# Activation of the second stage in turns, its low parts on VectorE, GpSimd left out

## The chip, the core and the metric

The kernel runs on one core of a Trainium2 chip. Its engines work side by side, each through its own queue in order: PE (TensorE, matmuls; PEld is its weight load), DVE (VectorE), ACT (ScalarE), POOL (GpSimd) and SP (SyncE, which here issues every DMA). They wait for each other by semaphores. The metric is the time of one execution in microseconds; the median of several runs is given.

## The reference

```python
def _attn_ref(q, k, v, g_q, g_k):          # q, k, v: (8, 12, 448, 64)
    q_n, k_n = (rmsnorm(q, g_q), rmsnorm(k, g_k))
    scores = scale * np.matmul(q_n, k_n.transpose(0, 1, 3, 2))
    attn = softmax(scores)
    return np.matmul(attn, v)

def _moe_ref(x, w_in, w_out):               # x: (3584, 768), w_in: (768, 2048), w_out: (2048, 768)
    h = x @ w_in
    g = h * np.cos(h)
    return (g @ w_out).astype(np.float32)
```

x is the attention output with its heads joined. All is fp32. The change lies in `h * cos(h)` and around it.

## The kernel before

Matmuls run on pairs of rounded fp32 numbers: each operand is split into a high part (a cast to fp32r) and a low part (the rest), and three matmuls (high-high, high-low, low-high) take the place of one.

The first part of the program, up to about 1007 us, is the attention of eight batches with `h = x @ w_in` of the batch before in between; h goes to DRAM (`h_out` copies it from PSUM on ScalarE, `h_store` writes it). Then comes the second stage, written out by a second `Plan`: sixteen blocks of `h` of the last batch (`ffn1_block`, 18 matmuls each), and then `g @ w_out`.

The second product runs over four pairs of batches (b0, b1). A pair is done in seven products of the Strassen-Winograd form, P1, P5, P6, P2, P7, P3, P4 in this order. Each product has four groups, g = 0 to 3; a group is a block of 18 matmuls on PE, with operands 128 x 896. So a pair is 28 blocks or 504 matmuls, and the stage has 112 blocks or 2016 matmuls. The four quarters A, Bq, C, Dq of the activation are held in `gq[(q, g)]`. For each quarter and group:

- `gl_load` (SP, L523): loads h.
- `g_turns` step 0 (ACT, L528): n = h/2pi + 12582912, which rounds; step 1 (POOL, L530): takes the constant off and multiplies by -C1.
- `g_reduce` steps 0 and 1 (DVE, L535 and L537): h minus n times 2pi in two pieces, into r.
- `g_cos` (ACT, L541 and L542): the absolute value, then the sine of pi/2 minus it.
- `g_mul` (DVE, L545): times h.

`g_sum` (DVE, L548) makes differences of quarters, 16 groups a pair. For each block, `g_split` makes the high part (ACT, L556) and the low part (POOL, L554); the two rings of buffers for these hold four blocks each, the rings of n and r two. `ffn2` (PE, L576 to L578) takes both. A product ends in PSUM banks, three of eight; `o_copy` (ACT, L586) or `o_add` (DVE, L589) takes them out into `outs`, and `y_store` (SP, L592) stores the results. P6 takes one bank that P5 had: its third output waits for the first `o_add` of P5. `w_place` (SP, L564) loads weights; P5, P2, P3 and P4 use the same slots one after another.

What stands in which order on an engine is set by `Plan.order`, a list scheduler: every `add(engine, cost, due, function, ...)` is an instruction with a cost and a due time, and on each engine the ready one with the earliest due time goes next. Each engine then follows its list without exception.

Of the kernel before, what the change touches and what calls it, by code (L numbers as in the profile page):

```python
# [10 lines left out]
F32 = mybir.dt.float32  # L11
F32R = mybir.dt.float32r
I32 = mybir.dt.int32
AF = mybir.ActivationFunctionType
ALU = mybir.AluOpType
AX = mybir.AxisListType
PSUM = bass.MemoryType.PSUM

MAGIC = 12582912.0
C1 = 6.28125  # L20
C2 = 2.0 * math.pi - C1

TINY_SQ = 3.4332275390625e-05**2

PE, ACT, DVE, POOL, SP = "PE", "ACT", "DVE", "POOL", "SP"


class Plan:
# [18 lines left out]
    def add(self, eng, cost, due, fn, *args, r=(), w=(), land=0.0, start=0.0, lead=None):  # L47
        n = len(self.parts)
        deps = set()
        for key in r:  # L50
            deps.update(self.writer.get(key, ()))
        for key in w:
            deps.update(self.writer.get(key, ()))
            deps.update(self.readers.get(key, ()))
        for key in (*r, *w):
            name, inst = key[0], key[1]
            if name in self.rings:
                self.users.setdefault((name, inst), []).append(n)
        for key in r:
            self.readers.setdefault(key, []).append(n)  # L60
        for key in w:
            self.writer[key] = [n]
            self.readers[key] = []
        deps.discard(n)
        self.parts.append((eng, cost, due, fn, args, deps, land))
        self.start.append(start)
        self.lead.append(self.LEAD * (eng == PE) if lead is None else lead)
# [59 lines left out]
def tile_attention_moe(  # L127
# [11 lines left out]
    nc = tc.nc  # L139
    NU = sd_in.shape[0]  # L140
    B, S, D = 8, kT.shape[2], 64
# [9 lines left out]
    NG = 2  # L151
# [26 lines left out]
    halfpi = cpool.tile([128, 1], F32, tag="halfpi", name="halfpi")  # L178
# [311 lines left out]
    phs = {}  # L490
# [19 lines left out]

    def h_out(b, fc):
        he = hes[(b, fc)] = epool.tile([128, S], F32, tag="he", name=f"he{b}_{fc}")
        nc.scalar.copy(he, phs.pop((b, fc))[:, :S])  # L513

    def h_store(b, fc):
        nc.sync.dma_start(h_d[b, fc], hes.pop((b, fc)))
# [3 lines left out]
    gq, gns, grs, gsp = {}, {}, {}, {}  # L520
# [1 line left out]
    def gl_load(b, q, g, f0):  # L522
        nc.sync.dma_start(gq[(q, g)], h_d[b, f0 : f0 + NG].rearrange("f p s -> p f s"))  # L523

    def g_turns(i, q, g, step):
        if step == 0:
            gns[i] = gpool.tile([128, NG, S], F32, tag="n", name=f"n{i}", bufs=RING2["n"])
            nc.scalar.activation(gns[i], gq[(q, g)], AF.Copy, bias=MAGIC, scale=1.0 / (2.0 * math.pi))  # L528
        else:
            nc.gpsimd.tensor_scalar(gns[i], gns[i], -MAGIC, -C1, op0=ALU.add, op1=ALU.mult)  # L530

    def g_reduce(i, q, g, step):
        if step == 0:
            r = grs[i] = gpool.tile([128, NG, S], F32, tag="r2", name=f"r2{i}", bufs=RING2["r2"])
            nc.vector.tensor_tensor(r, gq[(q, g)], gns[i], ALU.add)  # L535
        else:
            nc.vector.scalar_tensor_tensor(grs[i], gns.pop(i), C2 / C1, grs[i], op0=ALU.mult, op1=ALU.add)  # L537

    def g_cos(i):
        r = grs[i]  # L540
        nc.scalar.activation(r, r, AF.Abs)  # L541
        nc.scalar.activation(r, r, AF.Sin, bias=halfpi, scale=-1.0)  # L542

    def g_mul(i, q, g):
        nc.vector.tensor_tensor(gq[(q, g)], grs.pop(i), gq[(q, g)], ALU.mult)  # L545
# [4 lines left out]
    def g_split(n, q, g, lo):  # L550
        t = gpool.tile([128, NG, S], F32R, tag="glo" if lo else "ghi", name=f"g{lo}_{n}", bufs=RING2["ghi"])
        gsp[(n, lo)] = t
        if lo:
            nc.gpsimd.tensor_tensor(t, gq[(q, g)], gsp[(n, 0)].bitcast(F32), ALU.subtract)  # L554
        else:
            nc.scalar.copy(t, gq[(q, g)])  # L556

# [22 lines left out]
    outs = {}  # L580
# [2 lines left out]
        outs["t"] = xpool.tile([128, 12, S], F32, tag="xs", name="outs")  # L583

    def o_copy(bank, dst):
        nc.scalar.copy(outs["t"][:, dst], banks[bank][:, :S])  # L586

    def o_add(bank, src, dst):
        nc.vector.tensor_tensor(outs["t"][:, dst], banks[bank][:, :S], outs["t"][:, src], ALU.add)  # L589

    def y_store(b, oc, src):
        nc.sync.dma_start(out[oc * 128 : oc * 128 + 128, b * S : (b + 1) * S], outs["t"][:, src])  # L592
# [3 lines left out]
    add = plan.add  # L596
# [182 lines left out]
    RING2 = {"he": 2, "n": 2, "r2": 2, "ghi": 4, "glo": 4}  # L779
# [7 lines left out]
    add = plan.add  # L787
# [35 lines left out]
    for t in range(B // 2):  # L823
        b0, b1 = 2 * t, 2 * t + 1
        T = T0 + 7 * NGR * BLOCK * t

        def produce(q, b, f0, due):
            nonlocal made
            for g in range(NGR):
                i, made = made, made + 1  # L830
                e = due + BLOCK * g
                k, nk, rk = ("G", q, g), ("n", i), ("r2", i)
                add(SP, ISS, e - 34.0, gl_load, b, q, g, f0 + NG * g, r=[("hd", b, f0 + NG * g + j) for j in range(NG)],
                    w=[k], land=LAND)
                add(ACT, 0.95, e - 24.0, g_turns, i, q, g, 0, r=[k], w=[nk])
                add(POOL, 1.35, e - 23.0, g_turns, i, q, g, 1, w=[nk])
                add(DVE, 1.4, e - 21.0, g_reduce, i, q, g, 0, r=[k, nk], w=[rk])
                add(DVE, 1.1, e - 20.0, g_reduce, i, q, g, 1, r=[nk], w=[rk])
                add(ACT, 2.0, e - 18.0, g_cos, i, w=[rk])
                add(DVE, 1.15, e - 15.0, g_mul, i, q, g, r=[rk], w=[k])  # L840

        def combine(dst, a, c, due):
            for g in range(NGR):
                add(DVE, 1.15, due + BLOCK * g - 13.0, g_sum, dst, a, c, g, r=[("G", a, g), ("G", c, g)], w=[("G", dst, g)])

        DUE = {name: T + NGR * BLOCK * k for k, (name, *_) in enumerate(PRODUCTS)}
        produce(A, b0, 0, DUE["P1"])
        produce(Bq, b1, 0, DUE["P5"])
        produce(C, b1, HF, DUE["P6"])
        produce(Dq, b0, HF, DUE["P2"])  # L850
        role = {}
        for k, (name, q, w0, bk, opens, closes) in enumerate(PRODUCTS):
            d = DUE[name]
            if opens:
                role[bk] = [free.pop(0) for _ in range(3)]
            if t == 0 or name not in KEEP:
                for c in range(HF):
                    place_weights(name, w0, c, d - 14.0 + BLOCK / 2 * c if t else max(c, 2.0 * w0 + 2 * c))
            for g in range(NGR):
                n, n_split = n_split, n_split + 1  # L860
                e = d + BLOCK * g
                hk, lk = ("ghi", n), ("glo", n)
                add(ACT, 0.95, e - 9.0, g_split, n, q, g, 0, r=[("G", q, g)], w=[hk])
                add(POOL, 2.2, e - 8.0, g_split, n, q, g, 1, r=[("G", q, g), hk], w=[lk])
                wpos = (w0 + NG * g, w0 + NG * g + 1)
                add(PE, BLOCK, e, ffn2, n, g, wpos, tuple(role[bk]), opens,
                    r=[hk, lk] + [("wp", i) for i in wpos], w=[("y", i) for i in role[bk]])
            if name == "P1":
                combine(A, Bq, A, DUE["P5"])
            elif name == "P5":  # L870
                combine(Bq, C, Bq, DUE["P7"])
                combine(A, C, A, DUE["P6"])
            elif name == "P2":
                combine(Dq, Dq, A, DUE["P4"])
            e = d + NGR * BLOCK
            for o in range(3):
                y, s0 = ("y", role[bk][o]), 4 * o
                y_b, (p1, qq, u4, c11) = role[bk][o], [("o", s0 + j) for j in range(4)]
                if name == "P1":
                    add(ACT, 0.53, e - 4.0, o_copy, y_b, s0, r=[y], w=[p1])  # L880
                elif name == "P5":
                    add(DVE, 0.62, e - 4.0, o_add, y_b, s0, s0 + 1, r=[y, p1], w=[qq])
                elif name == "P6":
                    add(DVE, 0.62, e - 4.0, o_add, y_b, s0 + 1, s0 + 2, r=[y, qq], w=[u4])
                elif name == "P2":
                    add(ACT, 0.53, e - 4.0, o_copy, y_b, s0 + 3, r=[y], w=[c11])
                    add(SP, ISS, e, y_store, b0, o, s0 + 3, r=[c11], land=LAND)
                elif name == "P7":
                    add(DVE, 0.62, e - 4.0, o_add, y_b, s0 + 1, s0 + 1, r=[y], w=[qq])
                    add(SP, ISS, e, y_store, b1, 3 + o, s0 + 1, r=[qq], land=LAND)  # L890
                elif name == "P3":
                    add(DVE, 0.62, e - 4.0, o_add, y_b, s0 + 2, s0 + 2, r=[y], w=[u4])
                    add(SP, ISS, e, y_store, b1, o, s0 + 2, r=[u4], land=LAND)
                else:
                    add(DVE, 0.62, e - 4.0, o_add, y_b, s0, s0, r=[y], w=[p1])
                    add(SP, ISS, e, y_store, b0, 3 + o, s0, r=[p1], land=LAND)
            if closes:
                free += role[bk]
# [50 lines left out]
```

## Time and profile before

| | us |
|---|---|
| median of 3 runs | 1620.33 (1619.12 to 1623.3) |
| profiled execution | 1620.0 |
| its span, first to last instruction | 1618.2 |
| PE busy | 1423.6 (88%) |
| DVE busy | 1270.4 (79%) |
| POOL busy | 1076.2 (67%) |
| ACT busy | 986.5 (61%) |

The rows below come from one execution, so sums are made against 1620.0 and its span. A busy PE is not PE at its peak; what a stage could take is read from stretches in which PE does not pause. Rows of a timeline give the start, the duration, the engine, the line, the operation and in brackets the idle time before it with what ended it.

### The profile page before, as it was taken

To read this page: it belongs to the slowest core of one execution; us is meant where nothing else is said; L and a number is where in the kernel's file an instruction comes from. 1 tells how busy PE (TensorE), PEld (TensorE's weight loads), DVE (VectorE), ACT (ScalarE), POOL (GpSimd) and SP (SyncE) were. 2 spreads that over 40 slices of the span, in tenths; PEclk is the share of its full clock that TensorE was granted. 3 is DMA by queue.
4 is the path that set the end of the run, shared out by engine and by line. 5 is a ranking of instruction groups with operands and counts; after the bars stand their busy time and mean duration, and the time that the engine had idled before them with its cause. 6 is when DMAs were issued, how large, how long until landed. Compare 5 with 4: busy or idle time off the path is not lost. (4 is left out here: it accounts for less than half of the span.)

```text
span 1618.2 us, 22760 instructions
## 1 busy us (share of the span) xinstructions
PE 1423.6 (88%) x7392; PEld 1190.8 (74%) x7392; DVE 1270.4 (79%) x1983; ACT 986.5 (61%) x1922; POOL 1076.2 (67%) x799
## 2 busy tenths in 40 slices
PE   2778998999999999999999999977986897598599
PEld 1456777788788888888788887966965786497488
DVE  6778989887978788787866652597999799799931
ACT  4776776777777777767766654563555455355421
POOL 7777877768776786867774522346876577587743
PEclk9997999999999999999999999998998899799889
DMA  5436643656565656555553312872573374157234
GB/s 169 132 120 191 210 138 107 189 182 209 165 211 154 195 169 186 166 184 168 171 174 100 102 53 67 328 242 85 202 258 95 115 243 166 57 198 257 90 96 129
DMA packets 137383, 261.91 MB, mean 162 GB/s; under 512 B 22240, under 2 KB 92208, under 8 KB 137264
## 3 DMA queue, kind: packets, MB, share of 16 engines
q1 hardware_dynamic: 137264, 260.46, 50.1%
q8 instruction: 58, 0.95, 0.3%
q14 instruction: 61, 0.50, 0.1%
HBM read 197.66 MB, written 62.73 MB: 161 GB/s over the span
## 5 line engine op out<-in xcount | busy, mean ns | idle before, releaser
L554 POOL TENSOR_TENSOR g<-gq,g 128x896 fp32r<-128x896 f32 x112 | 289.1, 2586 | 143.7 <-ACT g L556 133.4
L576 PE MATMUL y<-g,wo 128*128 128x448 f32 x672 | 254.1, 378 | 61.7 <-DVE outs L589 44.8
L577 PE MATMUL y<-g,wo 128*128 128x448 f32 x672 | 256.2, 381 | 46.0 <-POOL g L554 45.9
L404 ACT ACTIVATE P<-S,sm 128x448 f32<-128x448 f32 x336 | 213.9, 641 | 89.5 <-DVE S L391 80.6
L501 PE MATMUL ph<-xs,wi 128*128 128x448 f32 x672 | 264.7, 394 | 3.0 <-ACT he L513 2.8
L438 ACT CAST hi<-PT 128x448 fp32r<-128x448 f32 x384 | 188.4, 536 | 112.9 <-PE PT L431 50.9
L578 PE MATMUL y<-g,wo 128*128 128x448 f32 x672 | 251.6, 374 | 0.0
L502 PE MATMUL ph<-xs,wi 128*128 128x448 f32 x672 | 247.9, 369 | 0.0
L503 PE MATMUL ph<-xs,wi 128*128 128x448 f32 x672 | 247.4, 368 | 0.0
L391 DVE TENSOR_SCALAR_CACHE_REDUCE S<-S,nr 128x448 f32<-128x448 f32 x336 | 219.0, 683 | 18.4 <-PE S L384 17.7
L446 DVE TENSOR_TENSOR lo<-PT,hi 128x448 fp32r<-128x448 f32 x288 | 166.1, 617 | 69.2 <-ACT hi L438 67.1
L576 PEld LDWEIGHTS y<-g,wo 128*128 128x128 f32 x672 | 130.5, 194 | 78.8 <-DVE outs L589 46.3
L431 PE MATMUL PT<-ident,P 128*128 128x128 f32 x1344 | 184.5, 278 | 0.8 <-ACT P L404 0.8
L577 PEld LDWEIGHTS y<-g,wo 128*128 128x128 f32 x672 | 130.5, 194 | 70.1 <-POOL g L554 59.0
L431 PEld LDWEIGHTS PT<-ident,P 128*128 128x128 f32 x1344 | 162.7, 143 | 17.3 <-issue 1.8
L541 ACT ACTIVATE r<-r 128x896 f32<-128x896 f32 x64 | 61.0, 953 | 187.5 <-DVE r L537 187.4
L556 ACT CAST g<-gq 128x896 fp32r<-128x896 f32 x112 | 104.2, 934 | 89.2 <-PE y L578 72.0
L458 PE MATMUL O<-hi,vs 128*128 128x448 f32 x384 | 135.0, 399 | 25.4 <-DVE hi L448 10.6
L307 POOL TENSOR_TENSOR r<-r,nhalf 128x14 f32<-128x14 f32 (+1 forms) x49 | 130.8, 2671 | 38.8 <-DVE r L303 35.6
L501 PEld LDWEIGHTS ph<-xs,wi 128*128 128x128 f32 x672 | 127.7, 190 | 29.9 <-issue 10.9
L548 DVE TENSOR_TENSOR gq<-gq,gq 128x896 f32<-128x896 f32 x64 | 112.8, 1769 | 40.8 <-POOL g L554 40.8
L535 DVE TENSOR_TENSOR r<-gq,n 128x896 f32<-128x896 f32 x64 | 119.0, 1859 | 32.7 <-POOL n L530 30.4
(83 smaller groups left out, 3108.9 us busy)
## 6 DMA issues: line engine op xcount, KB each, us to landing
wo<-wo_d SPq DMA_DIRECT2D x152, 384.0 KB
h_d<-he SPq DMA_DIRECT2D x128, 224.0 KB
gq<-h_d SPq DMA_DIRECT2D x64, 448.0 KB
sd<-sd SPq DMA_DIRECT2D x48, 448.0 KB
wo_d<-ao SPq DMA_DIRECT2D x56, 384.0 KB
vd<-v SPq DMA_DIRECT2D x96, 160.0 KB
qd<-qT SPq DMA_DIRECT2D x48, 256.0 KB
raw<-w_in SPq DMA_DIRECT2D x16, 768.0 KB
```

Of the source, the lines that this page charges most:

```text
L391: nc.vector.tensor_scalar(d["S", t][:, :S], d["S", t][:, :S], d["nr"][:, t : t + 1], None, op0=ALU.mult, op1=ALU.min, accum_out=d["sm"][:, ...
L404: nc.scalar.activation(tl(u, f"P{t}", [128, S], F32, "P"), d.pop(("S", t))[:, :S], AF.Exp, bias=sm[:, 1, t : t + 1], scale=-1.0, accum_out ...
L431: nc.tensor.transpose(pt[:, t * 128 : t * 128 + 128], src, ident)
L438: nc.scalar.copy(hi, pt[:, hh * S : hh * S + S])
L446: nc.vector.tensor_tensor(lo, src, hi.bitcast(F32), ALU.subtract)
L501: nc.tensor.matmul(ph[:, :S], whi, x2[:, 0, :], start=(cc == 0), stop=False)
L502: nc.tensor.matmul(ph[:, :S], whi, x2[:, 1, :], start=False, stop=False)
L503: nc.tensor.matmul(ph[:, :S], wlo, x2[:, 0, :], start=False, stop=(cc == NCC - 1))
L554: nc.gpsimd.tensor_tensor(t, gq[(q, g)], gsp[(n, 0)].bitcast(F32), ALU.subtract)
L576: nc.tensor.matmul(y, whi, hi[:, e], start=first and e == 0, stop=False, **more)
L577: nc.tensor.matmul(y, whi, lo[:, e], start=False, stop=False, **more)
L578: nc.tensor.matmul(y, wlo, hi[:, e], start=False, stop=last and e == NG - 1, **more)
```

## The change

The activation is kept in turns: `h_out` stores h/2pi. In the second stage ScalarE writes n = h/2pi + 0.25 as an integer, VectorE subtracts it, and one sine of 2pi r + pi/2 gives the cosine. L530 (GpSimd), L537 (VectorE) and L541 (ScalarE) are gone. The factor 2pi comes back in `o_copy` and `o_add`, which now multiply. The low part of each block moves from GpSimd to VectorE. The costs and due times in the plan change with it.

```diff
     def h_out(b, fc):
-        nc.scalar.copy(he, phs.pop((b, fc))[:, :S])
+        nc.scalar.activation(he, phs.pop((b, fc))[:, :S], AF.Copy, scale=1.0 / (2.0 * math.pi))
...
-    def g_turns(i, q, g, step):
-        if step == 0:
-            gns[i] = gpool.tile([128, NG, S], F32, tag="n", name=f"n{i}", bufs=RING2["n"])
-            nc.scalar.activation(gns[i], gq[(q, g)], AF.Copy, bias=MAGIC, scale=1.0 / (2.0 * math.pi))
-        else:
-            nc.gpsimd.tensor_scalar(gns[i], gns[i], -MAGIC, -C1, op0=ALU.add, op1=ALU.mult)
+    def g_turns(i, q, g):
+        gns[i] = gpool.tile([128, NG, S], I32, tag="n", name=f"n{i}", bufs=RING2["n"])
+        nc.scalar.activation(gns[i], gq[(q, g)], AF.Copy, bias=0.25, scale=1.0)
 
-    def g_reduce(i, q, g, step):
...
-            nc.vector.tensor_tensor(r, gq[(q, g)], gns[i], ALU.add)
-        else:
-            nc.vector.scalar_tensor_tensor(grs[i], gns.pop(i), C2 / C1, grs[i], op0=ALU.mult, op1=ALU.add)
+    def g_reduce(i, q, g):
+        r = grs[i] = gpool.tile([128, NG, S], F32, tag="r2", name=f"r2{i}", bufs=RING2["r2"])
+        nc.vector.tensor_tensor(r, gq[(q, g)], gns.pop(i), ALU.subtract)
 
     def g_cos(i):
-        r = grs[i]
-        nc.scalar.activation(r, r, AF.Abs)
-        nc.scalar.activation(r, r, AF.Sin, bias=halfpi, scale=-1.0)
+        nc.scalar.activation(grs[i], grs[i], AF.Sin, bias=halfpi, scale=2.0 * math.pi)
...
         if lo:
-            nc.gpsimd.tensor_tensor(t, gq[(q, g)], gsp[(n, 0)].bitcast(F32), ALU.subtract)
+            nc.vector.tensor_tensor(t, gq[(q, g)], gsp[(n, 0)].bitcast(F32), ALU.subtract)
...
     def o_copy(bank, dst):
-        nc.scalar.copy(outs["t"][:, dst], banks[bank][:, :S])
+        nc.scalar.activation(outs["t"][:, dst], banks[bank][:, :S], AF.Copy, scale=2.0 * math.pi)
 
     def o_add(bank, src, dst):
-        nc.vector.tensor_tensor(outs["t"][:, dst], banks[bank][:, :S], outs["t"][:, src], ALU.add)
+        nc.vector.scalar_tensor_tensor(
+            outs["t"][:, dst], banks[bank][:, :S], 2.0 * math.pi, outs["t"][:, src], op0=ALU.mult, op1=ALU.add
+        )
...
-                add(POOL, 2.2, e - 8.0, g_split, n, q, g, 1, r=[("G", q, g), hk], w=[lk])
+                add(DVE, 1.1, e - 8.0, g_split, n, q, g, 1, r=[("G", q, g), hk], w=[lk])
```

PE's order stays as it is. Three places on other engines show what moves. A name such as r or g with a number is one buffer; `g_35` is the part of block 35 (its low part where it is on DVE or POOL).

VectorE, second pair, the last instructions ahead of P5's three adds. Before:

```order
L537 SCALAR_TENSOR_TENSOR r_13313<-n_13258,r_13313 128x896
L545 TENSOR_TENSOR gq_1_11770<-r_13260,gq_1_11770 128x896
L548 TENSOR_TENSOR gq_0_11761<-gq_0_11765,gq_0_11761 128x896
L548 TENSOR_TENSOR gq_1_11762<-gq_1_11766,gq_1_11762 128x896
L545 TENSOR_TENSOR gq_2_11771<-r_13313,gq_2_11771 128x896
L535 TENSOR_TENSOR r_13378<-gq_3_11772,n_13318 128x896
L537 SCALAR_TENSOR_TENSOR r_13378<-n_13318,r_13378 128x896
L589 TENSOR_TENSOR outs<-y_11754,outs 128x448
```

The same place now (the lines of the changed kernel: L527 reduces, L533 multiplies, L536 subtracts quarters, L542 is the low part, L577 the add):

```order
L542 TENSOR_TENSOR g_35_13211<-gq_3_11760,g_35_13207 128x896
L536 TENSOR_TENSOR gq_3_11760<-gq_3_11768,gq_3_11760 128x896
L542 TENSOR_TENSOR g_36_13236<-gq_0_11757,g_36_13231 128x896
L533 TENSOR_TENSOR gq_3_11772<-r_13201,gq_3_11772 128x896
L536 TENSOR_TENSOR gq_1_11762<-gq_1_11766,gq_1_11762 128x896
L542 TENSOR_TENSOR g_37_13262<-gq_1_11758,g_37_13257 128x896
L536 TENSOR_TENSOR gq_2_11763<-gq_2_11767,gq_2_11763 128x896
L536 TENSOR_TENSOR gq_3_11764<-gq_3_11768,gq_3_11764 128x896
L542 TENSOR_TENSOR g_38_13288<-gq_2_11759,g_38_13283 128x896
L577 SCALAR_TENSOR_TENSOR outs<-y_11754,outs 128x448
```

Low parts stand among the quarters' work, three blocks ahead of the adds; between P4's adds and P5's there are 23 instructions in both programs, 8 of them low parts now, and P5's last low part, `g_35`, is the fifteenth.

GpSimd, the end of the first part and what follows. Before:

```order
L487 TENSOR_TENSOR xs<-xf_11666,xs 128x448
L530 TENSOR_SCALAR n_11827<-n_11827 128x896
L530 TENSOR_SCALAR n_11831<-n_11831 128x896
L530 TENSOR_SCALAR n_11893<-n_11893 128x896
L530 TENSOR_SCALAR n_11924<-n_11924 128x896
L554 TENSOR_TENSOR g_0_11954<-gq_0_11757,g_0_11928 128x896
L530 TENSOR_SCALAR n_11962<-n_11962 128x896
L554 TENSOR_TENSOR g_1_11994<-gq_1_11758,g_1_11986 128x896
```

Now:

```order
L483 TENSOR_TENSOR xs<-xf_11319,xs 128x448
L483 TENSOR_TENSOR xs<-xf_11518,xs 128x448
L483 TENSOR_TENSOR xs<-xf_11666,xs 128x448
L932 UNCONDITIONAL_BRANCH
L932 ISA
```

All 176 instructions of the second stage (64 of L530, 112 of L554) left this queue, which now ends with the first part's last split.

ScalarE, the beginning of the second stage, between the h copies `he_1` and `he_3`. Before:

```order
L513 COPY he_1_11854<-y_11750 128x448
L541 ACTIVATE r_11860<-r_11860 128x896
L542 ACT_TABLE_LOAD
L542 ACTIVATE r_11860<-r_11860,halfpi 128x896
L513 COPY he_2_11890<-y_11751 128x448
L528 ACTIVATE n_11893<-gq_2_11759 128x896
L541 ACTIVATE r_11864<-r_11864 128x896
L542 ACTIVATE r_11864<-r_11864,halfpi 128x896
L513 COPY he_3_11922<-y_11752 128x448
```

Now:

```order
L509 ACTIVATE he_1_11855<-y_11750 128x448
L530 ACT_TABLE_LOAD
L530 ACTIVATE r_11833<-r_11833,halfpi 128x896
L523 ACTIVATE n_11864<-gq_2_11759 128x896
L530 ACTIVATE r_11859<-r_11859,halfpi 128x896
L523 ACTIVATE n_11888<-gq_3_11760 128x896
L509 ACTIVATE he_2_11893<-y_11751 128x448
L530 ACTIVATE r_11868<-r_11868,halfpi 128x896
L523 ACTIVATE n_11900<-gq_0_11761 128x896
L530 ACTIVATE r_11895<-r_11895,halfpi 128x896
L509 ACTIVATE he_3_11926<-y_11752 128x448
```

More of the activation stands ahead of the copy `he_3`: four sines and five n now, two and three before. On VectorE 45 instructions lead up to and include P5's first low part; nine of them need nothing that ScalarE does after `he_3`.

More of the change, by code (lines that the diff above doesn't have):

```diff
@@ L17 @@
 PSUM = bass.MemoryType.PSUM
-MAGIC = 12582912.0
-C1 = 6.28125
-C2 = 2.0 * math.pi - C1
 TINY_SQ = 3.4332275390625e-05**2
@@ L523, in gl_load @@
         nc.sync.dma_start(gq[(q, g)], h_d[b, f0 : f0 + NG].rearrange("f p s -> p f s"))
-    def g_turns(i, q, g, step):
-        if step == 0:
-            gns[i] = gpool.tile([128, NG, S], F32, tag="n", name=f"n{i}", bufs=RING2["n"])
-            nc.scalar.activation(gns[i], gq[(q, g)], AF.Copy, bias=MAGIC, scale=1.0 / (2.0 * math.pi))
-        else:
-            nc.gpsimd.tensor_scalar(gns[i], gns[i], -MAGIC, -C1, op0=ALU.add, op1=ALU.mult)
-    def g_reduce(i, q, g, step):
-        if step == 0:
-            r = grs[i] = gpool.tile([128, NG, S], F32, tag="r2", name=f"r2{i}", bufs=RING2["r2"])
-            nc.vector.tensor_tensor(r, gq[(q, g)], gns[i], ALU.add)
-        else:
-            nc.vector.scalar_tensor_tensor(grs[i], gns.pop(i), C2 / C1, grs[i], op0=ALU.mult, op1=ALU.add)
+    def g_turns(i, q, g):
[4 more added lines that the diff above has]
+        nc.vector.tensor_tensor(r, gq[(q, g)], gns.pop(i), ALU.subtract)
     def g_cos(i):
-        r = grs[i]
-        nc.scalar.activation(r, r, AF.Abs)
-        nc.scalar.activation(r, r, AF.Sin, bias=halfpi, scale=-1.0)
+        nc.scalar.activation(grs[i], grs[i], AF.Sin, bias=halfpi, scale=2.0 * math.pi)
     def g_mul(i, q, g):
@@ L834, in produce @@
                     w=[k], land=LAND)
[L835 to L840, printed above, removed]
+                add(ACT, 0.95, e - 24.0, g_turns, i, q, g, r=[k], w=[nk])
+                add(DVE, 1.1, e - 22.0, g_reduce, i, q, g, r=[k, nk], w=[rk])
+                add(ACT, 1.05, e - 20.0, g_cos, i, w=[rk])
+                add(DVE, 1.1, e - 18.0, g_mul, i, q, g, r=[rk], w=[k])
         def combine(dst, a, c, due):
```

## The prediction

> **What bounds the kernel now.** I read the page first, then the busy time by stage.
>
> ```profile
> span 1618.2 us, 22760 instructions
> PE 1423.6 (88%) x7392; PEld 1190.8 (74%) x7392; DVE 1270.4 (79%) x1983; ACT 986.5 (61%) x1922; POOL 1076.2 (67%) x799
> ```
>
> By stage (length, then PE, PEld, DVE, ACT and POOL busy with their instructions, granted clock, DMA share, GB/s):
>
> ```profile
> 0.00:1006.80 1006.80, 923.93 (x5088) 749.24 (x5089) 780.71 (x1667) 687.96 (x1574) 679.78 (x619) 0.98 0.50 156
> ...
> 1066.60:1614.70 548.10, 440.43 (x2017) 387.67 (x2016) 451.23 (x290) 264.96 (x306) 367.25 (x163) 0.93 0.48 157
> ```
>
> Up to 1006.8 us the diff touches only the form of the h copies. The seven products take the last 548.1 us. How long would their 2016 matmuls need with nothing to wait for? Two stretches in which PE never paused give the rate.
>
> ```profile
> 1552.00:1610.00 58.00, 58.00 (x288) 53.76 (x287) 8.55 (x12) 14.71 (x17) 29.96 (x15) 1.00 0.48 145
> ...
> 1270.00:1321.00 51.00, 51.00 (x248) 46.31 (x247) 45.10 (x29) 28.85 (x34) 39.23 (x18) 1.00 0.60 198
> ```
>
> The first and the last matmul of the products, and the adds at the end:
>
> ```profile
> 1066.62 0.36 PE L576 MATMUL y<-g,wo 128*128 128x448 f32 x1
> ...
> 1613.51 1.84 DVE L589 TENSOR_TENSOR outs<-y,outs 128x448 f32<-128x448 f32 x3 [12.75 <-PE y L578]
> ...
> 1614.33 0.37 PE L578 MATMUL y<-g,wo 128*128 128x448 f32 x1
> ```
>
> 58.00/287 is 0.2021 us a matmul, 51.00/247 is 0.2065; why the middle of the stage is slower at the same granted clock the trace does not tell. So the products need 407.4 to 416.3 us, in the middle 411.9, and 548.1 - 411.9 = 136.2 us are lost. The waits say to what.
>
> ```profile
> ACT r L541 <- DVE r L537: 187.4, 52, 8.8
> ...
> PE y L577 <- POOL g L554: 45.9, 35, 2.9
> PE y L576 <- DVE outs L589: 44.8, 4, 12.7
> ...
> DVE gq L548 <- POOL g L554: 40.8, 13, 6.8
> ...
> PE y L576 <- ACT g L556: 15.9, 7, 9.3
> ...
> PE y L576 <- DMA wo<-wo_d: 0.7, 1, 0.7
> ```
>
> PE waits for three things made late: low parts, the adds that free a PSUM bank, high parts. Transfers cost it 0.7 us. The 12.7 us wait comes once in each pair, when P6 wants a bank of P5.
>
> ```profile
> 1248.06 0.36 PE L578 MATMUL y<-g,wo 128*128 128x448 f32 x1
> 1261.14 0.74 PE L576 MATMUL y<-g,wo 128*128 128x448 f32 x1 [12.72 <-DVE outs L589]
> 1261.68 0.57 PE L577 MATMUL y<-g,wo 128*128 128x448 f32 x1
> 1262.05 0.57 PE L578 MATMUL y<-g,wo 128*128 128x448 f32 x1
> ```
>
> And VectorE ahead of that release:
>
> ```profile
> 1217.14 1.07 DVE L548 TENSOR_TENSOR gq<-gq,gq 128x896 f32<-128x896 f32 x1
> ...
> 1258.35 1.08 DVE L535 TENSOR_TENSOR r<-gq,n 128x896 f32<-128x896 f32 x1
> 1259.46 1.09 DVE L537 SCALAR_TENSOR_TENSOR r<-n,r 128x896 f32<-128x896 f32 x1
> 1260.47 1.68 DVE L589 TENSOR_TENSOR outs<-y,outs 128x448 f32<-128x448 f32 x3
> ```
>
> After it, matmuls start every 0.37 us instead of 0.20 for a while: the wait is paid again in clock. The adds were late because 23 VectorE instructions stand between P4's adds and P5's, and these ran from 1217.14 to 1260.47: 1.88 us each. Why 1.88, when some take 1.08?
>
> ```profile
> 1026.83 1.09 DVE L535 TENSOR_TENSOR r<-gq,n 128x896 f32<-128x896 f32 x1 [4.94 <-POOL n L530]
> 1027.96 1.09 DVE L537 SCALAR_TENSOR_TENSOR r<-n,r 128x896 f32<-128x896 f32 x1
> ...
> 1245.06 2.98 DVE L537 SCALAR_TENSOR_TENSOR r<-n,r 128x896 f32<-128x896 f32 x1
> 1247.96 2.98 DVE L545 TENSOR_TENSOR gq<-r,gq 128x896 f32<-128x896 f32 x1
> ```
>
> ```profile
> 1244.92 5.06 POOL L554 TENSOR_TENSOR g<-gq,g 128x896 fp32r<-128x896 f32 x2 [4.92 <-ACT g L556]
> 1250.07 1.66 POOL L530 TENSOR_SCALAR n<-n 128x896 f32<-128x896 f32 x1
> 1251.81 5.66 POOL L554 TENSOR_TENSOR g<-gq,g 128x896 fp32r<-128x896 f32 x2
> ```
>
> The same instruction takes 1.09 us with GpSimd idle and 2.98 beside a GpSimd low part; between 1257.5 and 1260.5, GpSimd idle again, it is back at 1.08. VectorE is the bound of this stage, and GpSimd makes it so.
>
> **The change, part by part.** The prices:
>
> ```profile
> L535 DVE TENSOR_TENSOR r<-gq,n 128x896 f32<-128x896 f32 x64 | 119.0, 1859 | 32.7 <-POOL n L530 30.4 <-issue 0.4
> L545 DVE TENSOR_TENSOR gq<-r,gq 128x896 f32<-128x896 f32 x64 | 118.8, 1863 | 2.3 <-ACT r L542 2.3
> L537 DVE SCALAR_TENSOR_TENSOR r<-n,r 128x896 f32<-128x896 f32 x64 | 118.4, 1851 | 1.6
> L548 DVE TENSOR_TENSOR gq<-gq,gq 128x896 f32<-128x896 f32 x64 | 112.8, 1769 | 40.8 <-POOL g L554 40.8
> ...
> L556 ACT CAST g<-gq 128x896 fp32r<-128x896 f32 x112 | 104.2, 934 | 89.2 <-PE y L578 72.0 <-DVE gq L548 9.1 <-POOL g L554 5.4
> ...
> L528 ACT ACTIVATE n<-gq 128x896 f32<-128x896 f32 x64 | 60.4, 946 | 0.0
> ...
> L589 DVE TENSOR_TENSOR outs<-y,outs 128x448 f32<-128x448 f32 x60 | 34.0, 614 | 49.2 <-PE y L578 49.2
> ```
>
> VectorE loses the 64 instructions of L537 and gains 112 low parts. It has 119.0 + 118.8 + 118.4 + 112.8 + 34.0 = 503.0 us now. With GpSimd empty through the whole stage I price each of the 64 x 3 + 112 = 304 at 1.09 us: 331.4, plus 60 adds at 0.614, 368.2 us in all. The bounds of that price are 1.08 and 1.85; I take 1.09 because the rows with GpSimd idle say so, also at 1026, with ScalarE and the transfers at work. An add that now multiplies first I leave at 0.61 (L535 and L537 cost the same when alone); the integer operand I leave at nothing, bounded above by the 0.01 us between 1.08 and 1.09, since no row has this mix.
>
> Per pair that is 76 x 1.09 + 15 x 0.614 = 92.0 us against 504 matmuls, 101.9 to 104.1 us: PE becomes the bound. Is it so in each part? The densest stretch is the 23 instructions between P4's adds and P5's: 25.1 + 1.8 = 26.9 us against eight blocks of 18 matmuls, 29.1 to 29.7. So the adds stand ready 2 to 3 us early, and the 12.7 us wait goes, with its slow matmuls. The low parts now wait in VectorE's queue, for block n - 4 to free the buffer and for the high part (0.93 us), and what stands behind them waits too. P5's last low part is 15 instructions behind P4's adds: 16.4 + 1.8 = 18.2 us after P4's end, and wanted 7 blocks, 25.5 us, after it. Seven microseconds cover these handshakes. I leave nothing for steady state; bounds 0 and 6 us a pair (below).
>
> ScalarE loses L541, and its 187.4 us of waits behind L537. The scaled h copy and o_copy become activations; 946 against 934 ns bounds that by 12 ns x 112 = 1.3 us in the first stage, hidden, since the chip's end there is PE's.
>
> A stretch in which the transfers run at their fullest:
>
> ```profile
> 1030.00:1034.00 4.00, 4.00 (x22) 3.70 (x21) 0.05 (x1) 0.00 (x0) 0.00 (x0) 1.00 1.05 399
> ```
>
> The transfers stay, in less time: 157 GB/s x 548.1 us = 86 MB, over 415 us 207 GB/s. The worst place is P3 to P4, which reuse the same weight slots: two weights of 384 KB and one group of 448 KB for each block, 1.25 MB in 3.65 us, 341 GB/s, while this kernel has moved 399.
>
> SyncE's loads that waited for GpSimd's low part now wait for VectorE's, in the same places of the queue: nothing.
>
> The beginning is the one place where a stall may stay.
>
> ```profile
> 1034.22 0.53 ACT L513 COPY he<-y 128x448 f32<-128x448 f32 x1 [6.52 <-DMA h_d<-he]
> ```
>
> ScalarE's h copy waits for its store until 1034.2, and the change moves nothing that would end this sooner. From there VectorE has 36 of the 45 instructions up to the first low part of P5 to do: 1035 + 39.2 = 1074, wanted at 1066.6 + 72 matmuls = 1081.2. Eleven groups still hand over VectorE to ScalarE and back; half a microsecond each would eat 5.5 of these 7, and P5's first high part stands behind all sixteen h copies, each waiting for the store two before it. Bounds: 0, and the 9.3 us that PE waits there now. I take 3.
>
> The sum: 1066.6 + 411.9 + 3 + 3.5 (last matmul to end, as now) = 1485.0 us of span. The profiled execution took 1620.0 for 1618.2, so 1.8 more: **1487 us**. It is 0.3 us under the median of the runs, which changes nothing.
>
> Two rules of the Trainium skill bear on the price 1.09. "VectorE: DVE Perf Modes", section on rules for kernel authors, advises to keep the number of VectorE instructions small; here it rises from 316 to 364, and by that rule with the present mean of 1.85 us the sum would be 48 x 1.85 = 89 us more VectorE work. "SBUF — State Buffer", section "Who interferes with whom", says that a VectorE instruction with two inputs in SBUF and a GpSimd one that reads SBUF exclude each other for a whole instruction; by that rule the sum is the one above. The rows 1.09 and 2.98 agree with the second.
>
> **Rivals.** In the chain that ended last, the matmul of 1261.14 comes again two pairs on:
>
> ```profile
> 1540.38 0.74 PE y L576
> ```
>
> (a) The slow instructions are not GpSimd's doing, and the low parts come at 1.85 us: 76 x 1.85 + 9.2 = 149.8 us a pair. A pair takes (1540.4 - 1261.1)/2 = 139.6 now, so 10.2 x 4 = 41 us slower, 1661. It decides from (139.6 - 9.2)/76 = 1.72 us on. Against it are the rows above; for it, that no low part has run on VectorE from SBUF.
>
> (b) One queue for everything: handshakes of 0.5 us per block use 4 us of the 2 to 3 spare before P5's adds; P6 waits 1.5 us and runs slowly for some 4.5: 6 us a pair, 24 in all, 1508; with worse delays up to half of the 136 us stay, 1552. For it speaks that a low part holds up the reductions behind it. (c) Weights late at P4: at 300 GB/s four blocks' 5 MB take 16.6 us instead of 14.6, 2 us in three pairs, 1493. Against: 0.7 us of waits. (d) The beginning keeps its 9.3 us, and some 7 at the slow clock: 1487 - 3 + 16 = 1500. (e) No change in time, if something that I don't see paces the stage.
>
> **How the numbers follow.** My forecast (1478 to 1496 by the two matmul rates and 0 to 9 us of stall) has 0.63, (b) 0.15, (d) 0.10, (c) 0.07, (a) 0.03, (e) 0.02. The floor is 1066.6 + 407.4 + 3.5 + 1.8 = 1479; the range goes from 1477 into (b), to 1525. What can be told from no change is 0.3% (the runs lie 0.26% apart). Only (a) is slower.
>
> **What would show it.** VectorE's instructions of this stage at 1.08 to 1.13 us, none near 3, its busy time there near 368; no wait of PE for the adds at P6; the granted clock at 1.00 behind 1081; a pair in 102 to 104 us. Wrong it would be if VectorE's mean stays over 1.3 us, if PE waits for low parts in P1 and P5, or if waits for weights appear at P4.

## The result and the profile after

The changed kernel takes 1481.76 us (median of 4 runs, 1480.05 to 1482.66), against 1619.72 for the kernel before in the same comparison (4 runs, 1618.47 to 1623.3). The ratio is 0.9144, with a 95% interval of 0.9126 to 0.9161. The profiled execution took 1482.66 us for a span of 1480.9, so again 1.8 lie outside the span.

The first two lines of the page of the changed kernel:

```profile
span 1480.9 us, 22496 instructions
PE 1390.7 (94%) x7392; PEld 1180.6 (80%) x7392; DVE 1132.0 (76%) x2031; ACT 931.2 (63%) x1858; POOL 686.8 (46%) x623
```

By stage, with the columns as before: the first part, the products, and the second pair by itself.

```profile
0.00:1006.80 1006.80, 920.81 (x5079) 746.54 (x5080) 780.15 (x1667) 687.07 (x1572) 680.29 (x618) 0.98 0.50 156
1066.60:1477.40 410.80, 410.68 (x2027) 380.26 (x2025) 313.25 (x328) 203.04 (x234) 0.00 (x0) 1.00 0.64 206
...
1170.70:1272.80 102.10, 102.10 (x505) 94.64 (x504) 87.58 (x92) 58.02 (x66) 0.00 (x0) 1.00 0.68 223
```

The first part is as it was. In the products PE is busy from end to end, at a granted clock of 1.00, where before it was busy for 440 of 548 us at 0.93. VectorE needs 87.6 us of the 102.1 of the second pair, and GpSimd has nothing to do. The first and the last matmul of the products, from the timeline of PE:

```profile
1068.55 0.36 PE L564 MATMUL y<-g,wo 128*128 128x448 f32 x1
...
1476.92 0.36 PE L566 MATMUL y<-g,wo 128*128 128x448 f32 x1
```

So the products take 1477.28 - 1068.55 = 408.7 us, where they took 548.1. These 139.4 us are the whole gain; a beginning 1.9 us later takes a little back, and the span is 137.3 us shorter. The waits of the second stage, longest first:

```profile
ACT g L544 <- PE y L566: 163.0, 89, 2.8
DVE g L542 <- ACT g L544: 77.1, 71, 3.0
DVE outs L577 <- PE y L566: 13.3, 7, 11.3
```

No row of PE is left in this view: PE waits for nobody, and the others wait for it. ScalarE's high parts stand 89 times until a block of PE frees their buffer, and the low parts on VectorE wait behind them. These waits cost nothing, since they are those of engines ahead of the bound.

The groups of the stage on VectorE and ScalarE (count, busy time, mean ns of one):

```profile
L542 DVE TENSOR_TENSOR g<-gq,g 128x896 fp32r<-128x896 f32 x112 | 122.0, 1090 | 83.8 <-ACT g L544 83.4
...
L527 DVE TENSOR_TENSOR r<-gq,n 128x896 f32<-128x896 f32 x64 | 69.5, 1087 | 20.6 <-ACT n L523 19.2
L536 DVE TENSOR_TENSOR gq<-gq,gq 128x896 f32<-128x896 f32 x64 | 69.3, 1089 | 1.4
L533 DVE TENSOR_TENSOR gq<-r,gq 128x896 f32<-128x896 f32 x64 | 69.1, 1084 | 6.1 <-ACT r L530 3.1 <-DMA gq<-h_d 3.0
...
L523 ACT ACTIVATE n<-gq 128x896 int32<-128x896 f32 x64 | 60.2, 943 | 5.3 <-DMA gq<-h_d 5.3
...
L577 DVE SCALAR_TENSOR_TENSOR outs<-y,outs 128x448 f32<-128x448 f32 x60 | 34.7, 618 | 13.3 <-PE y L566 13.3
```

Every kind of VectorE instruction with two inputs in SBUF now takes 1.08 to 1.09 us, where the means were 1.77 to 1.86. The integer operand costs nothing (1087 ns), writing an integer on ScalarE costs nothing (943 against 946 ns), and an add that also multiplies costs 0.618 instead of 0.614 us.

### The profile page after: what moved, and what is told of

It reads as the page before. It is cut to its first block, busy times and chain, and to the rows that moved or that the text cites. A ratio compares the mean times of both kernels' runs of the same rounds, so it can differ in the third digit from the quotient of the medians.

```text
span 1480.9 us, 22496 instructions
## 1 busy us (share of the span) xinstructions
PE 1390.7 (94%) x7392; PEld 1180.6 (80%) x7392; DVE 1132.0 (76%) x2031; ACT 931.2 (63%) x1858; POOL 686.8 (46%) x623
## 4 chain that ended last, share of the span: by engine, by line
PE 79%; DVE 9%; ACT 4%; issue 2%; DMA 0%; POOL 0%; SPq 0%; POOLq 0%; ACTq 0%; DVEq 0%
PE O L454 9%; PE y L565 9%; PE y L564 9%; PE y L566 9%; PE PT L427 8%; PE ph L497 8%; PE ph L499 7%; PE ph L498 7%; PE S L380 7%; ACT hi L434 2%; DVE lo L442 2%; DVE S L387 2%; PE y L498 1%; PE y L499 1%; PE y L497 1%
## 5 line engine op out<-in xcount | busy, mean ns | idle before, releaser
L565 PE MATMUL y<-g,wo 128*128 128x448 f32 x672 | 245.5, 365 | 0.0
L564 PE MATMUL y<-g,wo 128*128 128x448 f32 x672 | 245.5, 365 | 0.0
L566 PE MATMUL y<-g,wo 128*128 128x448 f32 x672 | 245.5, 365 | 0.0
L544 ACT CAST g<-gq 128x896 fp32r<-128x896 f32 x112 | 105.7, 944 | 176.2 <-PE y L566 163.0
L542 DVE TENSOR_TENSOR g<-gq,g 128x896 fp32r<-128x896 f32 x112 | 122.0, 1090 | 83.8 <-ACT g L544 83.4
L454 PE MATMUL O<-hi,vs 128*128 128x448 f32 x384 | 134.8, 398 | 25.6 <-DVE hi L444 11.4
L497 PEld LDWEIGHTS ph<-xs,wi 128*128 128x128 f32 x672 | 127.4, 190 | 29.3 <-issue 10.9
L454 PE MATMUL O<-lo,vs 128*128 128x448 f32 x288 | 114.6, 410 | 27.3 <-DVE lo L442 26.2
L499 PEld LDWEIGHTS ph<-xs,wi 128*128 128x128 f32 x672 | 127.2, 189 | 11.5 <-POOL wi L230 0.4
L566 PEld LDWEIGHTS y<-g,wo 128*128 128x128 f32 x672 | 126.2, 188 | 10.0
L565 PEld LDWEIGHTS y<-g,wo 128*128 128x128 f32 x672 | 126.2, 188 | 10.0
L564 PEld LDWEIGHTS y<-g,wo 128*128 128x128 f32 x672 | 126.2, 188 | 10.0
```

Of the source, the lines that this page charges most:

```text
L454: nc.tensor.matmul(O, st, d.pop((what, kb, hh)), start=(kc + n == 0), stop=(kc + n == 4))
L497: nc.tensor.matmul(ph[:, :S], whi, x2[:, 0, :], start=(cc == 0), stop=False)
L499: nc.tensor.matmul(ph[:, :S], wlo, x2[:, 0, :], start=False, stop=(cc == NCC - 1))
L564: nc.tensor.matmul(y, whi, hi[:, e], start=first and e == 0, stop=False, **more)
L565: nc.tensor.matmul(y, whi, lo[:, e], start=False, stop=False, **more)
L566: nc.tensor.matmul(y, wlo, hi[:, e], start=False, stop=last and e == NG - 1, **more)
```

## The experiments

Three theories were set against each other.

- **L, the lock**: a VectorE instruction with two inputs in SBUF and a GpSimd instruction that reads SBUF exclude each other, so that a pair costs VectorE its own work and GpSimd's. The low part's move off GpSimd is then needed for the gain.
- **N**: only the number of instructions of the activation matters, and GpSimd's reads don't.
- **S**: any work of GpSimd slows VectorE, also work that only writes.

All runs are compared with the kernel before on the same chip, whose medians were 1620.89 to 1622.02 us. Differences to the changed kernel are taken from its 1481.76.

**The new activation alone, the low part still on GpSimd.** From the changed kernel:

```diff
-            nc.vector.tensor_tensor(t, gq[(q, g)], gsp[(n, 0)].bitcast(F32), ALU.subtract)
+            nc.gpsimd.tensor_tensor(t, gq[(q, g)], gsp[(n, 0)].bitcast(F32), ALU.subtract)
...
-                add(DVE, 1.1, e - 8.0, g_split, n, q, g, 1, r=[("G", q, g), hk], w=[lk])
+                add(POOL, 2.2, e - 8.0, g_split, n, q, g, 1, r=[("G", q, g), hk], w=[lk])
```

> The new activation, the low parts back on GpSimd. Theory L (a VectorE instruction with two inputs in SBUF and a GpSimd one that reads SBUF exclude each other, so the pair lasts as long as the sum of both at their lone durations, or as PE's 102.2 us): 48 x 1.09 on VectorE and 28 x 2.1 on GpSimd are 111 us, 9 us over PE in four pairs, about 1520 us; VectorE's mean about 1.8, GpSimd's about 2.7. Rival N (what counted was the shorter activation, three instructions less for each group): 1482 to 1490.

It took 1502.28 us, ratio 0.927 (0.925 to 0.929). Groups of the second stage (from 1000 us), and then the waits of PE:

```profile
L542 POOL TENSOR_TENSOR g<-gq,g 128x896 fp32r<-128x896 f32 x112 | 270.9, 2430 | 203.2 <-ACT g L544 200.3 <-DVE gq L536 2.9
...
L527 DVE TENSOR_TENSOR r<-gq,n 128x896 f32<-128x896 f32 x64 | 121.1, 1900 | 28.4 <-ACT n L523 26.8
L536 DVE TENSOR_TENSOR gq<-gq,gq 128x896 f32<-128x896 f32 x64 | 107.1, 1705 | 49.0 <-POOL g L542 48.5
```

```profile
PE y L565 <- POOL g L542: 8.4, 8, 1.4
PE y L564 <- DVE outs L577: 4.7, 3, 1.6
PE y L564 <- DMA wo<-wo_d: 2.2, 3, 1.0
```

VectorE's instructions are slow again as soon as the low parts are back on GpSimd, and PE waits again for low parts and for the adds, and a little for weights. It is 20 us above the changed kernel, not the 38 that L gave: the activation alone brings 120 us (1621.94 - 1502.28). But L's sum is not what bounds it. The stretch from P6's wait in the second pair to that in the third (length, then PE, PEld, VectorE, ScalarE and GpSimd busy):

```profile
1206.06:1315.54 109.48, 103.59 (x505) 94.28 (x505) 92.43 (x64) 57.28 (x67) 68.42 (x29) 1.00 0.63 208
```

VectorE is busy for 92.4 of 109.5 us and GpSimd for 68.4: neither is full. The products take 430.2 us, 21.5 more than the changed kernel's, and 15.3 of these are the three waits of PE above.

**The low part alone on VectorE, the old activation.** From the kernel before:

```diff
-            nc.gpsimd.tensor_tensor(t, gq[(q, g)], gsp[(n, 0)].bitcast(F32), ALU.subtract)
+            nc.vector.tensor_tensor(t, gq[(q, g)], gsp[(n, 0)].bitcast(F32), ALU.subtract)
...
-                add(POOL, 2.2, e - 8.0, g_split, n, q, g, 1, r=[("G", q, g), hk], w=[lk])
+                add(DVE, 1.1, e - 8.0, g_split, n, q, g, 1, r=[("G", q, g), hk], w=[lk])
```

> The old activation, the low parts on VectorE. Theory L: 92 x 1.09 + 9.2 on VectorE are 109.5 us a pair, and GpSimd's 16 x 0.94 of the remaining instruction add 15: 124.5, 22 over PE in four pairs, about 1570 us. Without mutual exclusion 109.5, about 1511. Rival N (the shorter activation is the gain): about 1620, as before.

It took 1533.42 us, ratio 0.945 (0.942 to 0.948). Groups of the second stage:

```profile
L554 DVE TENSOR_TENSOR g<-gq,g 128x896 fp32r<-128x896 f32 x112 | 127.8, 1141 | 35.1 <-ACT g L556 35.0
...
L548 DVE TENSOR_TENSOR gq<-gq,gq 128x896 f32<-128x896 f32 x64 | 81.2, 1280 | 0.3
...
L530 POOL TENSOR_SCALAR n<-n 128x896 f32<-128x896 f32 x64 | 77.2, 1206 | 371.1 <-ACT n L528 334.2 <-DVE g L554 30.5 <-DVE r L535 6.3
```

VectorE has 112 instructions more than before, and the kernel is 88 us faster (1621.94 - 1533.42): this refutes N, which had no change here. The time lies between the 1570 that L gave and the 1511 without exclusion, so L's price was too high here as well. With the little work that GpSimd keeps, the means fall from 1.77 to 1.86 us to 1.12 to 1.28. Both parts of the change bring much when made alone, 120 and 88 us, and 138 together: once PE is the bound, the rest of the saving has nothing left to shorten.

**GpSimd reads beside the changed kernel.** Nothing waits for this work; it subtracts a high part from itself, for every second block, into a buffer of its own.

```diff
+    def g_dummy(n):
+        hi = gsp[(n, 0)].bitcast(F32)
+        nc.gpsimd.tensor_tensor(dum, hi, hi, ALU.subtract)
...
+                if n % 2 == 0:
+                    add(POOL, 2.2, e - 7.0, g_dummy, n, r=[hk], w=[("dum", 0)])
```

> The changed kernel, and for every second block a GpSimd subtraction 128x896 of the high part from itself into a tile that nobody reads; the orders of PE, ScalarE and VectorE are the same. Theory L: 92.0 + 14 x 2.1 = 121.4 us a pair, 19 over PE in four pairs, about 1559 us; VectorE's mean in the stage 1.4 to 1.6. Rival N (GpSimd's work does not matter): 1482, VectorE at 1.09.

It took 1511.63 us, ratio 0.9328 (0.9308 to 0.9348). Groups, and the wait of PE for the adds:

```profile
L542 DVE TENSOR_TENSOR g<-gq,g 128x896 fp32r<-128x896 f32 x112 | 154.2, 1377 | 56.4 <-ACT g L544 56.3
L548 POOL TENSOR_TENSOR dum<-g 128x896 f32<-128x896 f32 x56 | 131.0, 2339 | 349.1 <-ACT g L544 348.8
```

```profile
PE y L568 <- DVE outs L581: 15.8, 3, 5.3
```

**GpSimd writes beside the changed kernel.** Instead of the subtraction, one of a single column and three fills of the same buffer, so that GpSimd writes SBUF for about as long but hardly reads it.

```diff
-        nc.gpsimd.tensor_tensor(dum, hi, hi, ALU.subtract)
+        nc.gpsimd.tensor_tensor(dum[:, 0, 0:1], hi[:, 0, 0:1], hi[:, 0, 0:1], ALU.subtract)
+        for _ in range(3):
+            nc.gpsimd.memset(dum[:, :, 1:], 0.0)
```

> As the run before, but GpSimd only writes: three memsets of 128x894 in place of the subtraction, behind a one-column subtraction that ties them to the block. Theory L with reads as what excludes: 1482 us, VectorE at 1.09, though GpSimd is about as busy. The Trainium skill, page SBUF - State Buffer, section Who interferes with whom, says that such a GpSimd instruction does not contend. Rival S (any GpSimd work slows VectorE): as the run with reads, about 1559.

It took 1483.43 us, ratio 0.9151 (0.9131 to 0.917), which is the changed kernel's time.

```profile
L550 POOL MEMSET dum<- 128x894 f32 x168 | 142.1, 846 | 6.4
L542 DVE TENSOR_TENSOR g<-gq,g 128x896 fp32r<-128x896 f32 x112 | 122.1, 1091 | 83.6 <-ACT g L544 83.3
```

131.0 us of GpSimd reads cost 30 us of time and lift the low part from 1.09 to 1.38 us; 142.1 us of GpSimd writes (beside 61.8 of one-column subtractions) cost nothing and leave it at 1.09. S falls, L's mechanism stands. VectorE's adds bear it out: they have one input in PSUM, and in the run with the low part on GpSimd 41 of the 60 lie wholly beside a GpSimd low part and still take 0.61 us. This is the rule of the Trainium skill, "SBUF — State Buffer", section "Who interferes with whom": a VectorE instruction with two SBUF inputs contends with a GpSimd instruction that reads SBUF, and not with one that only writes it. Both halves agree with these rows. L's price for the reads, 77 us, was again too high, and VectorE's mean over all large instructions is 1.30 us, below the 1.4 to 1.6 expected: of the 304, 46 take 2.45 to 2.58 us, for 56 reads.

**More work for VectorE, GpSimd empty.** Sums of a quarter with itself, into a buffer that nobody reads; 8 a pair (every second group), and 16:

```diff
+    def g_extra(q, g):
+        nc.vector.tensor_tensor(dum, gq[(q, g)], gq[(q, g)], ALU.add)
...
+                if g % 2 == 0:
+                    add(DVE, 1.1, e - 17.5, g_extra, q, g, r=[k], w=[("dum", 0)])
```

> The changed kernel, and 8 more VectorE additions 128x896 a pair (of a quarter to itself, into a tile that nobody reads), behind the multiplication of every second group. If PE is the bound and VectorE's queue counts by its sum: 84 x 1.09 + 9.2 = 100.8 us a pair under PE's 102.2, so 1482 to 1485 us. Rival (the handshakes in one queue had already used up VectorE's room): some 9 us a pair more, 1500 to 1518.

> The same with 16 more a pair, behind every group. By the sum: 92 x 1.09 + 9.2 = 109.5 us a pair, 7.3 over PE, in four pairs 29, about 1511 us, with waits of PE for low parts and for the adds and a lower granted clock. Rival (VectorE's work is hidden by the buffers anyway): 1482.

With 8 it took 1480.18 us (0.9124, 0.9094 to 0.9153): nothing, and PE has no wait. With 16 it took 1492.42 (0.9203, 0.9161 to 0.9244), 11 us more and not 29. PE's only wait there:

```profile
PE y L567 <- DVE outs L580: 7.2, 3, 4.4
```

VectorE had room for at least 8 more instructions a pair, so it was not at the edge; the wait that comes back first is that of P6 for P5's adds. The expectations came out too high here as in three of the runs before. One reason is that they took a pair's surplus four times, though it is paid almost only in the three stretches from one P6 to the next (8.5, 10.2 and 10.2 us over 102.1 with GpSimd's reads). Another is the price of VectorE's work. In the changed kernel's timeline one instruction begins 1.00 us after the other, though each is shown as 1.08 long:

```profile
1041.87 1.08 DVE L542 TENSOR_TENSOR g<-gq,g 128x896 fp32r<-128x896 f32 x1
1042.87 1.08 DVE L527 TENSOR_TENSOR r<-gq,n 128x896 f32<-128x896 f32 x1
```

Two more runs were made to see whether this 1.00 is the price: 32 sums a pair (two for each group), and GpSimd's reads for every block instead of every second.

> The changed kernel with 32 more VectorE instructions of 128x896 per pair (sums into a buffer that nobody reads), so that VectorE bounds the stage with GpSimd empty. Per pair it has 108 such instructions and 15 adds. If the price of one is its shown duration, 1.09 us (0.61 for an add), P6 comes every 108 x 1.09 + 15 x 0.61 = 126.9 us. If it is the 1.00 us between two starts in the changed kernel's trace (an add 1.68/3 = 0.56), it comes every 108 x 1.00 + 15 x 0.56 = 116.4 us. In time, with three pairs' worth of the surplus over 102.1 as in the run with GpSimd reads: 1482 + 3 x 24.8 = 1556 by the first, 1482 + 3 x 14.3 = 1525 by the second.

It took 1552.6 us, ratio 0.958 (0.9555 to 0.9606). P6's seventh matmul, the first of its third output, which waits for the adds, in the second and third pair; then that stretch by engine, and VectorE's waits in it:

```profile
1220.89 0.74 PE L567 MATMUL y<-g,wo 128*128 128x448 f32 x1 [5.51 <-DVE outs L580]
...
1345.45 0.74 PE L567 MATMUL y<-g,wo 128*128 128x448 f32 x1 [5.35 <-DVE outs L580]
```

```profile
1220.90:1345.40 124.50, 108.75 (x504) 97.64 (x504) 118.92 (x124) 58.96 (x66) 0.00 (x0) 0.94 0.53 183
```

```profile
DVE g L542 <- ACT g L544: 2.7, 2, 1.6
DVE r L527 <- ACT n L523: 1.9, 2, 1.3
```

A pair takes 124.6 us, and neither price gives that. By time 1552.6 is near the 1556 of the price 1.09, but for another reason: VectorE's own work is 118.9 us (124 instructions, 109 of them large), not 126.9, and the rest is waiting. 4.6 us of it are waits for ScalarE's high parts and n, which no price of an instruction holds. Some instructions do cost more than 1.00:

```profile
1275.09 1.08 DVE L542 TENSOR_TENSOR g<-gq,g 128x896 fp32r<-128x896 f32 x1
1276.09 1.08 DVE L533 TENSOR_TENSOR gq<-r,gq 128x896 f32<-128x896 f32 x1
1277.21 1.09 DVE L547 TENSOR_TENSOR dum<-gq 128x896 f32<-128x896 f32 x1
```

L533 does not need what L542 writes and begins 1.00 us after it; the sum L547 reads what L533 has just written and begins 1.12 after it. Over all large instructions that follow another without a wait, from 1000 us on, the mean distance is 1.04 us, in this kernel (386 of them) and in the changed one (199).

> The changed kernel with a GpSimd subtraction of 128x896 that reads the high part from SBUF for every block, 28 a pair (its result goes into a buffer that nobody reads). If VectorE's instructions with two inputs in SBUF and GpSimd's reads exclude each other, a pair is the sum of both: 76 x 1.00 + 28 x 2.1 = 134.8 us with the 15 adds beside GpSimd, 143.2 with the adds in the sum too; with 1.09 as VectorE's price 141.6 to 150.8. In time, with three pairs' worth of the surplus over 102.1: 1580 to 1605 by 1.00, 1600 to 1628 by 1.09. If it is only a fixed slowing (1.09 to 1.45, as the mean beside half as many reads), 76 x 1.45 + 8.4 = 118.6 a pair and 1531.

It took 1562.12 us, ratio 0.9641 (0.9625 to 0.9657), between the two expectations. VectorE's low parts, and P6's seventh matmul in the second and last pair:

```profile
L542 DVE TENSOR_TENSOR g<-gq,g 128x896 fp32r<-128x896 f32 x112 | 165.7, 1481 | 46.0 <-ACT g L544 45.3
```

```profile
1228.70 0.74 PE L568 MATMUL y<-g,wo 128*128 128x448 f32 x1 [8.23 <-DVE outs L581]
...
1483.54 0.74 PE L568 MATMUL y<-g,wo 128*128 128x448 f32 x1 [8.24 <-DVE outs L581]
```

A pair takes (1483.54 - 1228.70)/2 = 127.4 us, not 134.8 to 143.2. Not all of the 80 us over the changed kernel is exclusion: six high parts wait 13.9 us in all until a dummy read frees their buffer, and PE waits 7.7 us for weights. The timelines of GpSimd and of VectorE at one place show the size of the exclusion:

```profile
1263.69 4.17 POOL L548 TENSOR_TENSOR dum<-g 128x896 f32<-128x896 f32 x2 [1.83 <-ACT g L544]
```

```profile
1262.73 1.08 DVE L527 TENSOR_TENSOR r<-gq,n 128x896 f32<-128x896 f32 x1
1263.73 2.59 DVE L542 TENSOR_TENSOR g<-gq,g 128x896 fp32r<-128x896 f32 x1
1266.24 2.56 DVE L527 TENSOR_TENSOR r<-gq,n 128x896 f32<-128x896 f32 x1
1268.72 1.08 DVE L542 TENSOR_TENSOR g<-gq,g 128x896 fp32r<-128x896 f32 x1
```

Two GpSimd subtractions, two VectorE instructions, taking turns: VectorE's starts go from 1.00 us apart to 2.51 and 2.48. So one such read costs VectorE 1.5 us, not the 2.1 that the expectation took from the low part (the two inputs are the same here; the shortest one took 1.68 us). For a real low part the rows of 1245.06 and 1247.96 in the kernel before give 2.90 - 1.00 = 1.9 us.

With these prices, found afterwards (a large VectorE instruction 1.04 us, an add 0.56, a dummy read 1.5), the pairs in which VectorE is nearly full come out so; the measured pair is the distance between two of P6's waiting matmuls, and the last column is VectorE's busy time in it. The old activation's GpSimd step L530 has no price of its own here, so the two kernels with it are left out. The new activation with the low part on GpSimd is left out as well: its sum, 48 x 1.04 + 8.4 + 28 x 1.9 = 111.5, lies near its 109.5 and 107.6, but VectorE is busy for only 92.4 and 90.5 of them, so this proves nothing.

| kernel | VectorE | GpSimd's share | sum | measured pair | VectorE busy |
|---|---|---|---|---|---|
| changed, reads every second block | 76 x 1.04 + 8.4 | 14 x 1.5 | 108.4 | 112.3 | 106.1, 104.8 |
| changed, reads every block | 76 x 1.04 + 8.4 | 28 x 1.5 | 129.4 | 127.4 | 122.8 |
| changed, 32 sums more | 108 x 1.04 + 8.4 | 0 | 120.7 | 124.6 | 118.9 |

Sum and pair agree within 4 us, in part because two errors cancel. VectorE's busy time is 2 to 7 us below the sum; with reads this fits that not every read meets a large VectorE instruction. The pair is 4 to 8 us longer than the busy time, which is time in which VectorE waits.

## Why the prediction was right

1481.8 came where 1487 was forecast, inside 1477 to 1525, and the likeliest case is the one that happened.

**Right: GpSimd made VectorE the bound.** The rows of 1.09 against 2.98 were the reason, and rival (a) fell on them: no VectorE instruction of the stage is near 2 us now, and VectorE's groups in the stage sum to 122.0 + 69.5 + 69.3 + 69.1 + 34.7 = 364.6 us where 368.2 was forecast. That GpSimd's reads, and not its mere presence, do it is shown by the pair of runs with reads and with writes.

**Right: PE becomes the bound, and the P6 wait goes.** A pair takes 102.1 us (101.9 to 104.1 forecast), the granted clock is 1.00, and PE waits for nothing. The place that I had called the densest, P4's adds to P5's:

```profile
1170.35 1.68 DVE L577 SCALAR_TENSOR_TENSOR outs<-y,outs 128x448 f32<-128x448 f32 x3
1171.95 1.08 DVE L542 TENSOR_TENSOR g<-gq,g 128x896 fp32r<-128x896 f32 x1
...
1197.47 1.09 DVE L542 TENSOR_TENSOR g<-gq,g 128x896 fp32r<-128x896 f32 x1 [0.56 <-ACT g L544]
1198.86 1.84 DVE L577 SCALAR_TENSOR_TENSOR outs<-y,outs 128x448 f32<-128x448 f32 x3 [0.30 <-PE y L566]
```

VectorE stands at the adds 0.30 us before PE has made their input: it waits for PE, and P6 no longer for it. I had it ready 2 to 3 us early. The handshakes that rival (b) feared lie in between: five of the eight low parts wait for their high part, 0.42 to 0.56 us each, 2.4 us in all. But those high parts wait for PE to free their buffers (the 163.0 us above), so they follow the bound and do not delay it. (b) is what happens with VectorE fuller: the run with 16 sums more has the wait of 4.4 us back, and the one with 32 more 4.6 us of VectorE's time a pair in such handshakes.

**Right: the transfers.** They run at 206 GB/s over the stage (207 forecast), and no wait of PE for weights is left, at P4 neither; rival (c) did not occur in this kernel. In two of the experiments PE did wait for weights at P4: 2.2 us with the low part on GpSimd, 7.7 with GpSimd's reads for every block.

**Mis-sized: the stall in the beginning, 3 us taken, 0 found.** The h copy is released at 1036.25 and P5's first low part begins at 1073.84:

```profile
1036.25 0.54 ACT L509 ACTIVATE he<-y 128x448 f32<-128x448 f32 x1 [6.42 <-DMA h_d<-he]
```

```profile
1073.84 1.08 DVE L542 TENSOR_TENSOR g<-gq,g 128x896 fp32r<-128x896 f32 x1
```

From the copy's end, 1036.79, to the low part's, 1074.92, it took 38.1 us, where 39.2 without handshakes and up to 44.7 with them were forecast. PE wanted the low part at 1068.55 + 72 x 0.2027 = 1083.1, so 8.2 us were to spare instead of 1.7 to 7: the eleven handovers cost nearly nothing, and the instructions less than 1.09 each.

**Mis-sized: the matmul rate.** I took the middle of 0.2021 and 0.2065 us, 411.9; all of the products ran at 408.7/2016 = 0.2027. That is 3.2 us. The 0.2021 that I read as the faster rate was itself a little low: whole blocks of the faster kind take 0.2027 a matmul before the change too.

**Mis-sized, without effect: the price 1.09.** It is the duration of a VectorE instruction; the distance between two is 1.00 to 1.12, 1.04 in the mean. In the changed kernel this only adds to VectorE's slack (87.6 instead of 92.0 us a pair). In the experiments it made the expectations too high, together with the price of GpSimd's reads and, in the earlier ones, the surplus taken four times.

The sum, 1066.6 + 411.9 + 3 + 3.5 = 1485.0, against 1068.55 + 408.7 + 0 + 3.6 = 1480.9: 2 later, 3.2 less, 3 less. The later start is within what single executions do: with much the same first part, the first matmul of the products stands between 1064.9 and 1069.9 in the runs above. The limits of my likeliest case, 1478 and 1496, should have been 1479 and 1497 by the terms given; nothing hangs on it.

## What to carry to other kernels

When one engine's instructions come in two durations, look at what runs beside the long ones before counting instructions: here moving 112 instructions onto the stage's busiest engine made the kernel faster, because the engine that had them stood in its way when it read SBUF. Price a full queue by the distance between starts, not by the duration shown, and add the handshakes with the engines that feed it; they cost nothing as long as another engine is the bound, and some microseconds a round once it is the bound itself. Two changes that relieve the same bound do not add up: alone they brought 120 and 88 us, together 138, since no pair gets below PE's 102.1 us.

## What the runs showed of the hardware

- **VectorE's instructions overlap by 0.08 us** where the second doesn't need what the first wrote: starts 1.00 us apart at a shown duration of 1.08. They are 1.12 apart where it does, and also where it overwrites what the first has read: from 1188.01 to 1189.13 in the changed kernel, the low part `g_35` and the difference behind it. The Trainium skill, "VectorE: DVE Perf Modes", section "The DRAIN you can't avoid", has the next instruction wait until the pipeline is empty and says of one that is not held that it starts earlier; the starts at 1.00 agree with the second sentence.
- **The exclusion costs VectorE less than the whole GpSimd instruction as shown.** With 1.00 us as VectorE's own share, a low part that takes GpSimd 2.12 alone (1127.20 in the kernel before) costs VectorE 1.9 us, and a dummy read that takes at least 1.68 costs 1.5. The Trainium skill, "SBUF — State Buffer", section "SBUF: two separate sides", has the shared ports held for a whole instruction; the measured share is about nine tenths (1.9 of 2.12). What the rest is, no run here shows.
- **Matmuls have two spacings at a granted clock of 1.00.** The same stretch of the changed kernel and, in the second fence, of the one with the low part on GpSimd; in the third, a stretch of the run with 16 sums more, behind its wait of 4.4 us:

```profile
1090.00:1150.00 60.00, 60.00 (x297) 55.61 (x297) 44.89 (x48) 35.34 (x41) 0.00 (x0) 1.00 0.71 223
```

```profile
1090.00:1150.00 60.00, 60.00 (x292) 54.49 (x291) 42.65 (x32) 32.17 (x37) 37.55 (x17) 1.00 0.60 190
```

```profile
1419.00:1479.00 60.00, 60.00 (x292) 54.49 (x291) 40.38 (x43) 19.35 (x22) 0.00 (x0) 1.00 0.46 139
```

297 matmuls against 292 in 60 us, all without a pause. In every run here the spacing changes, between 0.2027 and about 0.2067 us a matmul, only where PE had paused; many pauses did not change it. In the changed kernel, in which PE has no pause in the products, the slower one never came; that is where the 3.2 us above come from. It does not need work of GpSimd, which is empty in the third fence. What causes it stays open.
